# Retention and a mixture of adapters on one core: load tiles on 256-byte addresses, the first quad whole, dummy matmuls while loads are under way

## The chip, the core and the metric

The kernel runs on one core of a Trainium2 chip. The metric is the device time of one execution in microseconds; lower is better. A core has five engines that run side by side and wait for each other through semaphores: TensorE (PE in the rows; its weight loads are PEld) multiplies from SBUF into PSUM, VectorE (DVE), ScalarE (ACT) and GpSimd (POOL) work on elements, and SyncE (SP) issues most of the DMAs that move data between HBM and SBUF. SBUF has 128 partitions; a tile's address is its byte offset in every partition. PSUM is handed out here in eight buffers of one bank each.

## What is computed

Eight sequences (batch) of 576 positions with eight heads of 64 elements go through a masked, decayed product of q, k and v, and the result through a mixture of eight rank-16 adapters, of which each token takes its best two.

```python
scores = scale * np.matmul(q, k.transpose(0, 1, 3, 2))
Dmat = np.where(rel >= 0, gamma[:, None, None] ** rel[None, :, :], 0.0)
ret = scores * Dmat[None, :, :, :]
attn_out = np.matmul(ret, v)                        # (8, 8, 576, 64)
x = attn_out.transpose(0, 2, 1, 3).reshape(4608, 512)
logits = x @ w_gate                                 # (4608, 8)
topk = np.argpartition(-logits, K, axis=1)[:, :K]   # K = 2
w = softmax of the two selected logits
delta[mask] += w[mask, k, None] * ((x[mask] @ A[e]) @ B[e])
return x + delta
```

## The kernel before

The positions are cut into four full chunks of 128 and one half chunk of 64, the eight batches into two quads of four. A full quad and chunk makes two units of two batches each (`units`, line 192), 16 full units in all, and the half chunk two units more, 18. Between chunks a decayed state P carries what k and v have summed up; so the work of a unit is always on 128 positions.

Each quad's q, k and v come as three tiles of 128 positions x (4 batches x 8 heads x 64) floats, 8 KB in each partition, from the pool `io` with three buffers each (`issue`, line 152). In HBM one row of 64 floats, 256 bytes, lies together. Quad 0 is loaded in nine DMAs (line 178): q and k of batch 0, of batch 1, then v of each, then batches 2 and 3 of q, k and v; the constants (`pack`) stand in between. Behind them come the adapter weights (`load_moe`: A in four DMAs of 64-byte pieces, the gate, B on GpSimd's queue), and then quad 1 in three DMAs. Later quads are issued two quads ahead, at the start of the first unit of a quad (line 513). All these DMAs but B, and all stores, are on SP's queue.

The stages of a unit, all written in one order by hand (each engine's `chain`, lines 73 to 87, keeps TensorE, VectorE and ScalarE in program order; GpSimd and SP are left to the scheduler):

- `scale_v` (line 203): GpSimd scales the unit's v in place, two instructions, for the unit after the current one.
- T (line 213): 16 transposes of q and 16 of k into PSUM, copied to `qT` and `kT` by ScalarE, the q of unit 0 by VectorE.
- S (line 268): 32 matmuls kT by qT; VectorE multiplies by the triangular mask into `rt`.
- Q (line 244): 32 matmuls of the state by qT, from chunk 1 on.
- U (line 315): 32 matmuls k by v, the state's update.
- R (line 341): 32 matmuls v by rt; VectorE scales into `xT`.
- Z (line 416): 16 matmuls of xT by `AW`, the adapters' A beside the gate (two versions, AW[1] a copy of AW[0] with its halves exchanged); then the choice of two on VectorE.
- W (line 443): gating on ScalarE and VectorE. B (line 386): 16 transposes of xT back into `po`. X (line 404): transposes of the gated z. Y (line 466): 4 matmuls by B on top of `po`, four copies to `osb` by ScalarE, two stores.

In the steady state TensorE's order in one step is S(t), T(t+1), B(t-1), Q(t), U(t), R(t), X(t-1), Z(t), Y(t-1). The opening is written apart (line 516): for unit 0 T and S are done batch by batch, then U and R; T(1) follows, and GpSimd copies AW[1]. Step 1 is S(1), T(2), U(1), R(1), Z(0), Z(1), and step 2 takes W, B, X and Y of both units 0 and 1. Names in brackets below, as S(2), are a stage and its unit.

Tiles are laid one after another in SBUF in the order of the pools: the constants first, then `io`, `work` and `moe` (which holds `osb`, the tile that stores leave from). Each tile's size is rounded up to 32 bytes; `warm` has 4 bytes and `pack` 464.

Of the kernel before, what the change touches and what calls it, by code (L numbers as in the profile page):

```python
# [18 lines left out]
def kernel(  # L19
# [17 lines left out]
    L = 64  # L37
# [42 lines left out]
    def mm(*args, **kw):  # L80
        chain("pe", nc.tensor.matmul(*args, **kw))  # L81
# [4 lines left out]
    def act(fn, **kw):  # L86
        chain("act", getattr(nc.scalar, fn)(**kw))  # L87

    cpool = ctx.enter_context(tc.tile_pool(name="consts", bufs=1))
    iop = ctx.enter_context(tc.tile_pool(name="io", bufs=3))  # L90
    wk = ctx.enter_context(tc.tile_pool(name="work", bufs=2))
    mo = ctx.enter_context(tc.tile_pool(name="moe", bufs=3))
    pp = ctx.enter_context(tc.tile_pool(name="pp", bufs=8, space=bass.MemoryType.PSUM))
# [22 lines left out]
    for g in range(2):  # L116
        gp.tensor_copy(
            out=trih[64 * g : 64 * g + 64], in_=tri[64 * g : 64 * g + 64, 64 * g : 64 * g + 64]
        )
    warm = cpool.tile([128, 1], FP32, tag="warm", name="warm")  # L120
    nc.vector.memset(warm, 0.0)
    nc.scalar.activation(out=warm, in_=warm, func=AFT.Sigmoid)
    pack = cpool.tile([128, NPK], FP32, tag="pack", name="pack")
# [28 lines left out]
    def issue(n):  # L152
        if n >= len(quads):
            return
        c, qd = quads[n]
        first = n == 0
        tl = [
            iop.tile([128, QUAD, H, Dh], FP32, tag=tag, name=tag) for tag in ("q32", "k32", "v32")
        ]
        if c == NFULL:  # L160
            for src, dst in zip((q, k, v), tl):
                for g in range(2):
                    nc.sync.dma_start(
                        out=dst[64 * g : 64 * g + 64, 0:2].rearrange("p s h d -> p (s h) d"),
                        in_=src[
                            QUAD * qd + 2 * g : QUAD * qd + 2 * g + 2, :, C * c : C * c + L, :
                        ].rearrange("s h j d -> j (s h) d"),
                    )
        def load(n, lo, hi):
            nc.sync.dma_start(  # L170
                out=tl[n][:, lo:hi].rearrange("p b h d -> p (b h) d"),
                in_=(q, k, v)[n][
                    QUAD * qd + lo : QUAD * qd + hi, :, C * c : C * c + C, :
                ].rearrange("b h j d -> j (b h) d"),
            )

        if first:
            for n, lo, hi in ((0, 0, 1), (1, 0, 1), (0, 1, 2), (1, 1, 2), (2, 0, 1), (2, 1, 2)):
                load(n, lo, hi)
                if (n, lo) == (1, 1):  # L180
                    nc.sync.dma_start(out=pack, in_=dr_pack.ap())
            for n in range(3):
                load(n, 2, 4)
            load_moe()
        elif c < NFULL:
            for n in range(3):
                load(n, 0, 4)
        for sl in range(2):
            nat[(c, qd, sl)] = [x[:, 2 * sl : 2 * sl + 2] for x in tl]
# [7 lines left out]
    def rows(g):  # L197
        return slice(64 * g, 64 * g + 64)
# [11 lines left out]
                op=ALU.mult,  # L210
            )

    def stage_T(t, bs=(0, 1)):

        q32, k32, v32 = nat[units[t]]
        s = st.setdefault(t, {})
        n = len(bs)
        for src, nm in ((q32, "qT"), (k32, "kT")):
            if bs[0] == 0:
                s[nm] = wk.tile([128, 2, HP, C], FP32, tag=nm, name=nm)  # L220
            dst = s[nm]
            ps = [pp.tile([128, HP, n, L], FP32, tag="pb", name=f"p{nm}") for _ in range(2)]
            for hp in range(HP):
                for b in bs:
                    for g in range(2):
                        mm(
                            ps[g][:, hp, b - bs[0], :],
                            lhsT=src[rows(g), b, 2 * hp : 2 * hp + 2, :],
                            rhs=id64[rows(g), :],
                            is_transpose=True,  # L230
                            start=True,
                            stop=True,
                        )
            for g in range(2):
                if is_full(t):
                    o = dst[:, bs[0] : bs[-1] + 1, :, rows(g)].rearrange("p b a i -> p a b i")
                else:
                    o = dst[:, g].rearrange("p a (b i) -> p a b i", b=2)
                if t == 0 and nm == "qT":
                    vec("tensor_copy", out=o, in_=ps[g])  # L240
                else:
                    act("copy", out=o, in_=ps[g])
# [22 lines left out]
                            skip_group_check=True,  # L265
                        )

    def stage_S(t, bs=(0, 1)):
        s = st[t]
        rt = s.setdefault("rt", {})  # L270
        if not is_full(t):
            ps = [pp.tile([128, HP, 2, L], FP32, tag="pb", name=f"pe{ho}") for ho in range(2)]
            for hp in range(HP):
                for y in range(2):
                    for x in range(2):
                        for ho in range(2):
                            mm(
                                ps[ho][rows(x), hp, y, :],
                                lhsT=s["kT"][rows(ho), x, hp, rows(y)],
                                rhs=s["qT"][rows(ho), x, hp, rows(y)],  # L280
                                start=(hp == 0 and y == 0),
                                stop=True,
                                skip_group_check=True,
                            )
            for ho in range(2):
                r = wk.tile([128, HP, 2, L], FP32, tag=f"rh{ho}", name=f"rh{ho}")
                vec("tensor_tensor", 
                    out=r.rearrange("p a y i -> p (a y) i"),
                    in0=ps[ho].rearrange("p a y i -> p (a y) i"),
                    in1=trih.unsqueeze(1).broadcast_to((128, HP * 2, L)),  # L290
                    op=ALU.mult,
                )
                rt[ho] = r
            return
        for b in bs:
            ps = [pp.tile([128, HP, C], FP32, tag="pb", name=f"ps{ho}") for ho in range(2)]
            for hp in range(HP):
                for ho in range(2):
                    mm(
                        ps[ho][:, hp, :],  # L300
                        lhsT=s["kT"][rows(ho), b, hp, :],
                        rhs=s["qT"][rows(ho), b, hp, :],
                        start=(hp == 0),
                        stop=True,
                        skip_group_check=True,
                    )
            for ho in range(2):
                r = wk.tile([128, HP, C], FP32, tag=f"rt{ho}", name=f"rt{ho}", bufs=4)
                vec(
                    "tensor_tensor", out=r, in0=ps[ho],  # L310
                    in1=tri.unsqueeze(1).broadcast_to((128, HP, C)), op=ALU.mult,
                )
                rt[(b, ho)] = r
# [152 lines left out]
    def stage_Y(t):  # L466
        c, qd, sl = units[t]
        s = st.pop(t)
        po = s["po"]
        osb = mo.tile([128, 2, HP, 2, Dh], FP32, tag="osb", name="osb", bufs=3)  # L470
        bv = Bcat.rearrange("p (a o d) -> p a o d", a=HP, o=2)
        for cc in range(2):
            for g in range(2):
                mm(
                    po[cc][:, g, :, :],
                    lhsT=s["zT"][:, g, :],
                    rhs=bv[:, :, cc ^ g, :],
                    start=False,
                    stop=True,
                    skip_group_check=True,  # L480
                )
        for cc in range(2):
            for g in range(2):
                act("copy", out=osb[:, g, :, cc ^ g, :], in_=po[cc][:, g])
        of = osb.rearrange("p g a o d -> p g (a o d)")
        for g in range(2):
            for x in range(1 if c < NFULL else 2):
                bt = 2 * sl + g if c < NFULL else 2 * g + x
                n0 = S * (QUAD * qd + bt) + C * c
                if c < NFULL:  # L490
                    nc.sync.dma_start(out=out[n0 : n0 + C, :], in_=of[:, g, :])
                else:
                    nc.sync.dma_start(out=out[n0 : n0 + L, :], in_=of[rows(x), g, :])
# [17 lines left out]
    for t in range(NU):  # L511
# [2 lines left out]
        if t + 1 < NU:  # L514
            scale_v(t + 1)
        if t == 0:
            for b in range(2):
                stage_T(0, (b,))
                stage_S(0, (b,))
            stage_Q(0)  # L520
            stage_U(0)
            stage_R(0)
            stage_T(1)
            for ho in range(2):
                gp.tensor_copy(out=AW[1][rows(ho)], in_=AW[0][rows(1 - ho)])
            continue
        done = [0, 1] if t == 2 else [t - 1] if t > 2 else []
        if not is_full(t):
# [11 lines left out]
        stage_R(t)  # L540
        for u in done:
            stage_X(u)
        if t == 1:
            stage_Z(0)
        stage_Z(t)
        for u in done:
            stage_Y(u)
# [34 lines left out]
```

## Time and profile before

| | us |
|---|---|
| median of 3 runs (lowest to highest) | 216.16 (215.51 to 217.12) |
| the profiled execution, its time | 216.31 |
| the profiled execution, its span | 214.6 |
| TensorE busy in the span | 185.4 (86%) |
| VectorE, ScalarE, GpSimd busy | 108.1, 72.9, 58.3 |
| HBM read, written | 28.91 MB, 9.44 MB |

The span runs from the first to the last instruction of the program; the time holds what lies around it as well. Rows give times in us from the span's start. [...] An engine's busy time is the time its instructions were being worked on; matmuls are pipelined, so that the mean of one is longer than the step from one to the next.

### The profile page before, as it was taken

The numbers are of one execution on the slowest core, as the hardware profiler recorded it, in microseconds if no ns is written. First come the engines' busy times: TensorE is split into PE (matmuls) and PEld (weight loads), VectorE is DVE, ScalarE is ACT, GpSimd is POOL, SyncE is SP. The second block draws the span as 40 slices with busy tenths as digits, with TensorE's granted clock in tenths as the row PEclk, the third lists the DMA queues.
The fourth block names the chain that finished last, engine by engine and source line by source line (L and its number), as shares of the span: only waits on it lengthen the run. The fifth ranks groups of instructions, "written<-read, shape, count | busy, mean of one in ns | idle before, by whom it ended". The sixth has DMA issues, their size and how long they took to land.

```text
span 214.6 us, 8018 instructions
## 1 busy us (share of the span) xinstructions
PE 185.4 (86%) x3564; PEld 169.3 (79%) x3564; DVE 108.1 (50%) x269; ACT 72.9 (34%) x200; POOL 58.3 (27%) x68
## 2 busy tenths in 40 slices
PE   1688328999999989999999998999899999998850
PEld 1577318989998979898989997999799999987730
DVE  0333401576756545756565656555655546443620
ACT  2202122143633333333434342435243525163141
POOL 4353200702504501721180029004732041200000
PEclk9999955999999999999999999999999999999996
DMA  6997999999999989779988698999981642020235
GB/s 137 232 220 87 208 219 219 196 228 205 218 221 322 226 194 215 256 161 233 230 204 224 145 252 193 259 203 230 266 206 46 167 91 99 5 101 3 104 77 118
DMA packets 57010, 38.73 MB, mean 180 GB/s; under 512 B 30736, under 2 KB 52368, under 8 KB 56976
## 3 DMA queue, kind: packets, MB, share of 16 engines
q1 hardware_dynamic: 56832, 38.09, 78.7%
q8 instruction: 28, 0.46, 0.9%
q0 software_dynamic: 144, 0.13, 0.4%
q14 instruction: 6, 0.05, 0.1%
HBM read 28.91 MB, written 9.44 MB: 179 GB/s over the span
## 4 chain that ended last, share of the span: by engine, by line
PE 70%; DMA 10%; SPq 9%; DVE 3%; issue 2%; POOL 2%; ACT 1%; ACTq 0%
PE px L81 19%; PE pz L81 15%; PE ps L81 12%; PE po L81 8%; PE pu L81 8%; SPq L170 6%; DMA k<-in_k_dram 5%; DMA v<-in_v_dram 4%; PE pkT L81 3%; SPq L139 3%; PE pqT L81 3%; POOL v L206 2%; PE pzt L81 2%; DVE rt L84 1%; ACT osb L87 1%
## 5 line engine op out<-in xcount | busy, mean ns | idle before, releaser
L206 POOL TENSOR_TENSOR v<-v,pack 128x512 f32<-128x512 f32 x36 | 36.5, 1043 | 82.0 <-DMA v<-in_v_dram 81.9
L84 DVE TENSOR_TENSOR rt<-ps,tri 128x512 f32<-128x512 f32 x64 | 39.8, 683 | 20.3 <-PE ps L81 20.3
L81 PE MATMUL pz<-AW,xT 128*128 128x136 f32 x288 | 37.2, 283 | 1.1 <-DVE xT L84 1.1
L81 PE MATMUL ps<-qT,kT 64*128 64x128 f32 x512 | 35.0, 288 | 3.7 <-ACT kT L87 2.4
L81 PEld LDWEIGHTS ps<-qT,kT 64*128 64x128 f32 x512 | 31.6, 196 | 7.1 <-ACT kT L87 4.2
L81 PEld LDWEIGHTS pz<-AW,xT 128*128 128x128 f32 x288 | 34.5, 190 | 1.6 <-DVE xT L84 1.5
L81 PE MATMUL px<-rt,v 128*64 128x128 f32 x512 | 33.1, 285 | 0.0
L87 ACT COPY osb<-po 128x256 f32<-128x256 f32 x72 | 21.5, 390 | 30.0 <-PE po L81 30.0
L81 PEld LDWEIGHTS px<-rt,v 128*64 128x64 f32 x512 | 30.0, 145 | 0.0
L87 ACT COPY qT<-pqT 128x512 f32<-128x512 f32 x34 | 18.3, 590 | 33.9 <-PE pqT L81 33.9
L84 DVE TENSOR_TENSOR xT<-px,asc 128x512 f32<-128x512 f32 x36 | 24.7, 691 | 9.5 <-PE px L81 8.4
L339 POOL TENSOR_TENSOR P<-pn,gdec 128x512 f32<-128x512 f32 x12 | 15.2, 1271 | 38.6 <-DVE pn L84 38.6
L87 ACT COPY zT<-pzt 128x256 f16<-128x256 f16 x18 | 6.6, 372 | 54.5 <-PE pzt L81 54.5
L87 ACT COPY kT<-pkT 128x512 f32<-128x512 f32 (+1 forms) x38 | 19.9, 585 | 10.5 <-PE pkT L81 10.5
L81 PE MATMUL pu<-v,k 128*64 128x64 f32 x512 | 20.3, 236 | 2.8 <-issue 1.4
L81 PEld LDWEIGHTS pu<-v,k 128*64 128x64 f32 x512 | 18.0, 148 | 5.7 <-POOL v L206 3.1
L81 PE MATMUL pqT<-id,q 64*128 64x64 f32 x288 | 13.4, 236 | 8.0 <-DMA q<-in_q_dram 8.0
L81 PEld LDWEIGHTS pqT<-id,q 64*128 64x128 f32 x288 | 12.4, 150 | 8.5 <-issue 8.4
L84 DVE TENSOR_TENSOR pn<-pu,P 128x512 f32<-128x512 f32 x12 | 8.3, 692 | 20.2 <-PE pu L81 20.2
L81 PE MATMUL pkT<-id,k 64*128 64x64 f32 x288 | 13.7, 234 | 4.2 <-DMA k<-in_k_dram 4.1
L81 PE MATMUL po<-id,xT 64*128 64x64 f32 x288 | 15.9, 229 | 0.7 <-DVE rt L84 0.3
L81 PE MATMUL px<-qT,P 64*64 64x128 f32 (+1 forms) x512 | 15.9, 261 | 0.6 <-issue 0.6
(39 smaller groups left out, 127.5 us busy)
## 6 DMA issues: line engine op xcount, KB each, us to landing
out_dram<-osb SPq DMA_DIRECT2D x32, 256.0 KB, 3.9
q<-in_q_dram SPq DMA_DIRECT2D x6, 256.0 KB, 5.5
k<-in_k_dram SPq DMA_DIRECT2D x6, 256.0 KB, 4.8
v<-in_v_dram SPq DMA_DIRECT2D x6, 256.0 KB, 4.8
out_dram<-osb SPq DMA_DIRECT2D x8, 128.0 KB, 2.4
q<-in_q_dram SPq DMA_DIRECT2D x1, 512.0 KB, 6.2
k<-in_k_dram SPq DMA_DIRECT2D x1, 512.0 KB, 7.5
v<-in_v_dram SPq DMA_DIRECT2D x1, 512.0 KB, 7.8
```

What stands on the lines that cost most here:

```text
L81: chain("pe", nc.tensor.matmul(*args, **kw))
L84: chain("dve", getattr(nc.vector, fn)(**kw))
L87: chain("act", getattr(nc.scalar, fn)(**kw))
L139: nc.sync.dma_start(out=AW[0][:, dt, 0:ER].rearrange("p (e r) -> p e r", e=E), in_=moe_A[:, 128 * dt : 128 * dt + 128, :].rearrange("e d r ...
L170: nc.sync.dma_start(out=tl[n][:, lo:hi].rearrange("p b h d -> p (b h) d"), in_=(q, k, v)[n][QUAD * qd + lo : QUAD * qd + hi, :, C * c : C ...
L206: nc.gpsimd.tensor_tensor(out=vv[:, b], in0=vv[:, b], in1=gv[:, 0 if is_full(t) else 1].unsqueeze(2).broadcast_to((128, H, Dh)), op=ALU.mult,)
L339: nc.gpsimd.tensor_tensor(out=Pt, in0=pn, in1=gdec, op=ALU.mult)
```

## The change

Two pools are opened ahead of the constants: `padp` with `warm`, now 32 floats instead of 1, and then `io`, followed by a new pool `outp` that holds `osb`. The constants come behind them. Quad 0 is loaded in three DMAs, one for each of q, k and v, with `pack` behind k. T and S lose their form for single batches; the q of unit 1 is copied by VectorE too. `spin` issues dummy matmuls of a zeroed fp16 tile, 128 x 128 by 128 x 512, into a PSUM tile that nothing reads: 12 ahead of T(0) and 12 between its q and its k transposes. The opening is then T(0), T(1), S(0), S(1), U(0), R(0), U(1), R(1), the copy of AW[1], Z(0), Z(1), T(2), and step 1 is empty but for its scaling of v. From step 2 on the order is the same.

```diff
--- before.py
+++ after.py
@@ -86,8 +86,13 @@
     def act(fn, **kw):
         chain("act", getattr(nc.scalar, fn)(**kw))
 
+
+
+    padp = ctx.enter_context(tc.tile_pool(name="padp", bufs=1))
+    warm = padp.tile([128, 32], FP32, tag="warm", name="warm")
+    iop = ctx.enter_context(tc.tile_pool(name="io", bufs=3))
+    outp = ctx.enter_context(tc.tile_pool(name="outp", bufs=3))
     cpool = ctx.enter_context(tc.tile_pool(name="consts", bufs=1))
-    iop = ctx.enter_context(tc.tile_pool(name="io", bufs=3))
     wk = ctx.enter_context(tc.tile_pool(name="work", bufs=2))
     mo = ctx.enter_context(tc.tile_pool(name="moe", bufs=3))
     pp = ctx.enter_context(tc.tile_pool(name="pp", bufs=8, space=bass.MemoryType.PSUM))
@@ -117,7 +122,15 @@
         gp.tensor_copy(
             out=trih[64 * g : 64 * g + 64], in_=tri[64 * g : 64 * g + 64, 64 * g : 64 * g + 64]
         )
-    warm = cpool.tile([128, 1], FP32, tag="warm", name="warm")
+    idle = cpool.tile([128, 512], FP16, tag="idle", name="idle")
+    nc.vector.memset(idle, 0.0)
+    spare = pp.tile([128, 512], FP32, tag="pb", name="spare")
+
+    def spin(n):
+
+        for _ in range(n):
+            mm(spare, lhsT=idle[:, 0:128], rhs=idle, start=True, stop=True)
+
     nc.vector.memset(warm, 0.0)
     nc.scalar.activation(out=warm, in_=warm, func=AFT.Sigmoid)
     pack = cpool.tile([128, NPK], FP32, tag="pack", name="pack")
@@ -175,12 +188,10 @@
             )
 
         if first:
-            for n, lo, hi in ((0, 0, 1), (1, 0, 1), (0, 1, 2), (1, 1, 2), (2, 0, 1), (2, 1, 2)):
-                load(n, lo, hi)
-                if (n, lo) == (1, 1):
+            for n in range(3):
+                load(n, 0, 4)
+                if n == 1:
                     nc.sync.dma_start(out=pack, in_=dr_pack.ap())
-            for n in range(3):
-                load(n, 2, 4)
             load_moe()
         elif c < NFULL:
             for n in range(3):
@@ -210,21 +221,20 @@
                 op=ALU.mult,
             )
 
-    def stage_T(t, bs=(0, 1)):
+    def stage_T(t, pause=0):
 
         q32, k32, v32 = nat[units[t]]
         s = st.setdefault(t, {})
-        n = len(bs)
         for src, nm in ((q32, "qT"), (k32, "kT")):
-            if bs[0] == 0:
-                s[nm] = wk.tile([128, 2, HP, C], FP32, tag=nm, name=nm)
-            dst = s[nm]
-            ps = [pp.tile([128, HP, n, L], FP32, tag="pb", name=f"p{nm}") for _ in range(2)]
+            if nm == "kT":
+                spin(pause)
+            dst = s[nm] = wk.tile([128, 2, HP, C], FP32, tag=nm, name=nm)
+            ps = [pp.tile([128, HP, 2, L], FP32, tag="pb", name=f"p{nm}") for _ in range(2)]
             for hp in range(HP):
-                for b in bs:
+                for b in range(2):
                     for g in range(2):
                         mm(
-                            ps[g][:, hp, b - bs[0], :],
+                            ps[g][:, hp, b, :],
                             lhsT=src[rows(g), b, 2 * hp : 2 * hp + 2, :],
                             rhs=id64[rows(g), :],
                             is_transpose=True,
@@ -233,10 +243,10 @@
                         )
             for g in range(2):
                 if is_full(t):
-                    o = dst[:, bs[0] : bs[-1] + 1, :, rows(g)].rearrange("p b a i -> p a b i")
+                    o = dst[:, :, :, rows(g)].rearrange("p b a i -> p a b i")
                 else:
                     o = dst[:, g].rearrange("p a (b i) -> p a b i", b=2)
-                if t == 0 and nm == "qT":
+                if t < 2 and nm == "qT":
                     vec("tensor_copy", out=o, in_=ps[g])
                 else:
                     act("copy", out=o, in_=ps[g])
@@ -265,7 +275,7 @@
                             skip_group_check=True,
                         )
 
-    def stage_S(t, bs=(0, 1)):
+    def stage_S(t):
         s = st[t]
         rt = s.setdefault("rt", {})
         if not is_full(t):
@@ -292,7 +302,7 @@
                 )
                 rt[ho] = r
             return
-        for b in bs:
+        for b in range(2):
             ps = [pp.tile([128, HP, C], FP32, tag="pb", name=f"ps{ho}") for ho in range(2)]
             for hp in range(HP):
                 for ho in range(2):
@@ -467,7 +477,7 @@
         c, qd, sl = units[t]
         s = st.pop(t)
         po = s["po"]
-        osb = mo.tile([128, 2, HP, 2, Dh], FP32, tag="osb", name="osb", bufs=3)
+        osb = outp.tile([128, 2, HP, 2, Dh], FP32, tag="osb", name="osb")
         bv = Bcat.rearrange("p (a o d) -> p a o d", a=HP, o=2)
         for cc in range(2):
             for g in range(2):
@@ -514,15 +524,22 @@
         if t + 1 < NU:
             scale_v(t + 1)
         if t == 0:
-            for b in range(2):
-                stage_T(0, (b,))
-                stage_S(0, (b,))
-            stage_Q(0)
-            stage_U(0)
-            stage_R(0)
+            spin(12)
+            stage_T(0, pause=12)
             stage_T(1)
+            stage_S(0)
+            stage_S(1)
+            for u in range(2):
+                stage_Q(u)
+                stage_U(u)
+                stage_R(u)
             for ho in range(2):
                 gp.tensor_copy(out=AW[1][rows(ho)], in_=AW[0][rows(1 - ho)])
+            for u in range(2):
+                stage_Z(u)
+            stage_T(2)
+            continue
+        if t == 1:
             continue
         done = [0, 1] if t == 2 else [t - 1] if t > 2 else []
         if not is_full(t):
@@ -540,8 +557,6 @@
         stage_R(t)
         for u in done:
             stage_X(u)
-        if t == 1:
-            stage_Z(0)
         stage_Z(t)
         for u in done:
             stage_Y(u)
```

## Rows read from the trace of the kernel before

**Rows 1.** Busy time by engine in stretches: engines, PEclk, DMA share, GB/s.
```profile
0.00:19.60 19.60, 12.46 (x138) 11.21 (x140) 5.80 (x12) 2.78 (x6) 8.63 (x22) 1.00 1.03 180
19.60:26.50 6.90, 2.95 (x60) 2.62 (x56) 2.82 (x5) 2.05 (x4) 2.22 (x3) 1.00 0.91 168
26.50:36.70 10.20, 5.03 (x76) 4.78 (x78) 0.69 (x1) 2.15 (x4) 0.00 (x0) 0.50 1.11 218
36.70:41.90 5.20, 5.20 (x58) 4.90 (x54) 2.79 (x6) 0.24 (x2) 4.04 (x4) 1.00 0.98 193
41.90:205.00 163.10, 157.85 (x3223) 144.68 (x3222) 94.80 (x239) 62.57 (x175) 43.45 (x40) 1.00 0.76 183
```

**Rows 2.** The chain that ended last: start us, us, what.
```profile
21.28 11.37 DMA k<-in_k_dram
```

**Rows 3.** TensorE's timeline, opening: start, us, operation xcount [idle before <-releaser].
```profile
4.20 0.69 PE L81 MATMUL pqT<-id,q 64*128 64x64 f32 x8 [4.20 <-DMA q<-in_q_dram]
5.28 0.69 PE L81 MATMUL pkT<-id,k 64*128 64x64 f32 x8 [0.39 <-DMA k<-in_k_dram]
6.70 2.08 PE L81 MATMUL ps<-qT,kT 64*128 64x128 f32 x16 [0.73 <-ACT kT L87]
...
15.49 3.63 PE L81 MATMUL px<-rt,v 128*64 128x128 f32 x32
...
27.96 1.12 PE L81 MATMUL pqT<-id,q 64*128 64x64 f32 x16 [3.78 <-DMA q<-in_q_dram]
32.79 1.12 PE L81 MATMUL pkT<-id,k 64*128 64x64 f32 x16 [3.71 <-DMA k<-in_k_dram]
...
41.89 2.06 PE L81 MATMUL ps<-qT,kT 64*128 64x128 f32 x32
...
46.94 1.15 PE L81 MATMUL pu<-v,k 128*64 128x64 f32 x32
```

**Rows 4.** Stretches chosen for the DMA traffic, columns as in rows 1.
```profile
2.00:4.00 2.00, 0.00 (x0) 0.00 (x0) 0.00 (x0) 0.29 (x2) 1.30 (x4) 1.00 1.01 229
...
17.00:22.00 5.00, 3.50 (x52) 3.02 (x50) 1.38 (x2) 1.98 (x4) 2.38 (x3) 1.00 0.64 60
...
23.00:24.00 1.00, 1.00 (x22) 0.99 (x18) 0.68 (x2) 0.00 (x0) 0.00 (x0) 1.00 1.04 293
24.00:26.00 2.00, 0.19 (x4) 0.00 (x0) 1.81 (x4) 0.00 (x0) 0.00 (x0) 1.00 1.11 219
...
68.00:70.00 2.00, 2.00 (x38) 1.83 (x34) 1.52 (x3) 0.00 (x0) 2.00 (x3) 1.00 1.03 361
```

**Rows 5.** One steady unit in the chain that ended last.
```profile
61.73 0.44 PE po L81 x4
62.17 1.99 PE ps L81 x32
64.16 0.50 PE pqT L81 x16
...
66.98 1.08 PE pu L81 x32
68.06 1.75 PE px L81 x32
...
70.03 1.91 PE pz L81 x16
```

**Rows 6.** The timeline of ScalarE and VectorE, opening.
```profile
20.98 1.09 ACT L87 COPY kT<-pkT 128x512 f32<-128x512 f32 x2
...
23.32 2.48 DVE L84 TENSOR_TENSOR rt<-ps,tri 128x512 f32<-128x512 f32 x4 [3.39 <-PE ps L81]
```

**Rows 7.** GpSimd's timeline, opening.
```profile
18.51 2.04 POOL L206 TENSOR_TENSOR v<-v,pack 128x512 f32<-128x512 f32 x2 [4.62 <-DMA v<-in_v_dram]
```

**Rows 8.** TensorE's waits, 42 to 205 us: waited for, us, times, longest.
```profile
PE pu L81 <- issue: 1.4, 3, 0.7
...
PE pu L81 <- POOL v L206: 0.9, 1, 0.9
```

## The prediction

> **What bounds the kernel now.** I cut the span by stages first [rows 1]. From 41.9 to 205.0 us TensorE is busy for 157.85 of 163.1 us at the full granted clock: that stretch is bound by TensorE, one unit after the other, and only 5.2 us in it are idle. Before 41.9 it is busy for 12.46 of 19.6, 2.95 of 6.9 and 5.03 of 10.2 us. The first fifth of the span is where time lies.
>
> The chain that ended last says what this opening waits for [rows 2]: from 21.28 to 32.66 us it is the load of k of the second quad. In TensorE's own order [rows 3] unit 2's q transposes start at 27.96 and its k transposes at 32.79, each when its load lands, and unit 1's second half (U, R), both Z and S(2) follow them. S(2) starts at 41.89. Everything behind S(2) is the same program in both kernels, so I forecast where S(2) starts and shift the rest.
>
> The loads are not waiting to be issued: they run at a plateau. The stretch 24 to 26 us moves 219 GB/s with the DMA engines' share at 1.11, while stores of 2 KB rows move 361 GB/s in 68 to 70 us [rows 4]. So the engines can do more than the loads get from them. The load pieces are 256 B (one row of 64 floats).
>
> The clock is the third part. S(0)'s first half (16 matmuls, half of S) takes 2.08 us at 6.70, and S(2), with 32, takes 2.06 at 41.89; R(0) takes 3.63 us [rows 3], R in the steady stretch 1.75 [rows 5]. [...]
>
> **The change part by part.** All sums are against the profiled execution: span 214.6 us, time 216.31, so 1.7 us lie around the span; it is 0.15 above the median 216.16.
>
> *Addresses.* Summing the tile sizes (each rounded up to 32 B), the q, k and v tiles of before start 128 B past a multiple of 256, osb 224 B past; after, both pools start on multiples. A 256 B piece then no longer lies across two 256 B blocks. No row shows an aligned load. From below it gains nothing: 219 GB/s. From above it is the stores' 361. Just after an idle stretch the same unaligned loads ran at 293 GB/s (23 to 24 us) before they fell to the plateau [rows 4]: reading and sending can go that fast until something behind them fills. I take 293, the row between. A tensor of a quad (4 batches x 8 heads x 128 rows x 256 B = 1.049 MB) then takes 3.6 us, against 4.8 at 219 and 2.9 at 361. For osb I take nothing: stores are off the chain except in the last 9 us, with no row to price them.
>
> [...]
>
> *First quad whole.* Data starts at 2.0 us. The first 256 KB at 229 GB/s [rows 4] are over at 3.15, and TensorE starts on them at 4.20 [rows 3]: 1.05 us from last byte to use. Six small and three larger loads become three. q is usable at 2.0 + 3.6 + 1.05 = 6.6 and k at K = 10.2 (before, first halves at 4.20 and 5.28). With the pack (0.2) v is usable at 14.0. The 64 B pieces of A and the gate follow; before, that stretch (17 to 22 us) moved 60 GB/s [rows 4], and I charge the same 5.0 us. Then q, k, v of quad 1 are usable at 22.7, 26.3, 29.8.
>
> *Stage by stage.* Prices at the full clock come from one steady unit [rows 5]: T 0.5 for q and as much for k, S 2.0, U 1.1, R 1.75, Z 1.9. From K on TensorE has T(0)k and T(1) (1.5); S(0) then waits for the kT copies (1.1 on ScalarE, [rows 6]): start K + 2.0. S(0), S(1): to K + 6.0. U, R, U, R (5.7): K + 11.7. Two Z: K + 15.5. T(2): K + 16.5. New here: S(2) now stands right behind T(2), where before U(1), R(1) and Z hid T(2)'s copies; two pairs of 1.1 us on ScalarE, the first pair half covered, make S(2) K + 18.3 = 28.5.
>
> What must be ready beside it. VectorE: eight masks of 0.62 us (2.48 for four, [rows 6]) end by K + 8, R(1) needs them from K + 9.9; hidden. POOL: scaling a unit takes 2.04 us [rows 7], so v of unit 0 is ready at 14.0 + 2.0 = 16.1, and U(0) wants it at K + 6.0 = 16.2: no room, any us later is a us on the end. AW's copy ends near 20.4, Z(0) wants it at 21.9. T(2) wants k at 26.2 and has it at 26.3. U(2) comes 5.05 us after S(2) [rows 3], at 33.6, and v of quad 1 is scaled for it at 31.9. The DMAs moved on SP's queue (pack ahead of v, the MoE loads behind) keep their order against quad 1; the stores come later and are passed by nothing.
>
> *Keeping the array busy.* A 128-row fp16 matmul of 256 columns costs 0.11 us (0.44 for four, [rows 5]), so 512 columns 0.22, at the lower level 0.44. Twelve from about 1.3 us on at the lower level end at 6.6, just when q lands: free. Twelve more behind T(0)q, 2.6 us at the full clock, end at 9.9 before K: free. If the clock is still low they end near 13 and T(0)k is 2.8 us late.
>
> *Sum.* S(2) at 28.5 for 41.9: 13.4 us. In the TensorE-bound stretch the idle time ahead of U is 1.4 us ("issue") and 0.9 (scaled v) [rows 8]; lighter DMA traffic may take some of it: between 0 and 2.3, I take 1.0. Span 214.6 - 13.4 - 1.0 = 200.2, time 201.9; the 0.15 to the median is inside its spread. Forecast 202.0. At 361 GB/s K is 8.9, S(2) 27.2, with all 2.3 us: 199.3.
>
> What is late next: nothing on the DMA side. A quad's loads (10.8 us) and its stores (1.05 MB at 361: 2.9) fill 14 of the 21 us that two units take, and TensorE is the bound to the end.
>
> **The rivals.**
> 1. *Loads no faster.* For: no row of a load above 293, the plateau may be HBM's. Against: the stores' 361, and the overshoot after idling. Then K is 12.7, v scaled at 19.8, Z(1) done at 29.3, and T(2) waits for k at 32.79 as now, there being the same bytes ahead of it. S(2) 0.5 + 1.1 + 0.2 later, 34.6: 7.3 us gained, no stall removed. Time 209.0.
> 2. *The first dummies don't raise the clock*, and it rises near 19.6 as it seems to do now. For: rows of 0 to 19 us at half speed [rows 3] through several us of work. Against: that work was broken by waits up to 13 us. Price: 2.8 us for the second dozen, and 6.6 us of wall to 19.6 that do half the work, 3.3. Time 208.
> 3. *Slower: the clock stays low through the whole opening.* [...] For: 26.5 to 36.7 us at 0.50 [rows 1]. Against: that fall followed waits for loads, and after K the new order has none over 1 us.
>
> The change not doing what it says would be rival 1 (addresses) or 2 (array).
>
> **How the numbers follow.** Forecast 0.66, holding 199.3 (and a little under, 198.5, for the tail's stores) to 204.5; rival 1 0.15; rival 2, whole or in part, 0.12; rival 3 0.05; within 1%, the bound of what a measurement of this kernel can tell from no change, 0.02, by half of rival 3. Faster by over 1%: 0.66 + 0.15 + 0.12 = 0.93. The range from 198.5 to 208.5 holds the forecast and rival 2, and leaves out rival 3 and most of rival 1.
>
> **What would show it.** Right: load stretches of the opening near 290 GB/s with the DMA share not above now; T(0)k near 10, S(1) over by 17, S(2) near 28.5; S at 2.0 us for 32 matmuls from the first one; no clock row at 0.50 between 10 and 195 us; POOL's scaling of unit 0 ending near U(0)'s start; 41.9 to 205 repeated 13 us earlier with under 5 us idle. Wrong: a plateau of 219 again and S(2) tied to k's landing at 33 (rival 1); S(0) at 4 us (rivals 2, 3); or a new wait in the steady stretch, above all on osb, a PSUM buffer or scaled v.

## The result and the profile after

| | before | after |
|---|---|---|
| median, us (lowest to highest) | 216.03 (215.51 to 217.12) | 204.17 (203.81 to 206.74) |
| profiled execution: time, span | 216.31, 214.6 | 203.81, 202.1 |
| S(2) starts at | 41.89 | 29.82 |
| S(2) to the end of the span | 172.7 | 172.3 |
| DMA queue of loads and stores, share of 16 engines' span | 78.7% | 66.0% |

The ratio of the times is 0.947, 95% interval [0.9385, 0.9555]: 11.9 us less, where 14 were forecast, inside the range. Ratios, here and below, are formed from undisturbed executions alone, so the quotient of two medians can differ from them a little. Of the profiled span's 12.5 us, 12.1 come from the earlier start of S(2) and 0.4 from behind it.

TensorE's timeline of the opening (start, us, operation, tiles xcount, idle before and its releaser) answers to [rows 3]:

```profile
1.26 5.30 PE L81 MATMUL spare<-idle 128*128 128x512 f16 x12 [1.26 <-DVE warm L134]
7.17 0.71 PE L81 MATMUL pqT<-id,q 64*128 64x64 f32 x16 [0.60 <-DMA q<-in_q_dram]
7.82 2.76 PE L81 MATMUL spare<-idle 128*128 128x512 f16 x12
11.25 0.71 PE L81 MATMUL pkT<-id,k 64*128 64x64 f32 x16 [0.67 <-DMA k<-in_k_dram]
...
13.12 3.84 PE L81 MATMUL ps<-qT,kT 64*128 64x128 f32 x64
...
17.67 1.04 PE L81 MATMUL pu<-v,k 128*64 128x64 f32 x28 [0.43 <-POOL v L217]
...
27.66 0.71 PE L81 MATMUL pkT<-id,k 64*128 64x64 f32 x16
29.82 2.06 PE L81 MATMUL ps<-qT,kT 64*128 64x128 f32 x32 [1.45 <-ACT kT L87]
```

The first dozen dummies take 5.30 us, 0.44 each, the second 2.76: the whole first dozen ran at half the speed of the second, though the profile's clock row says 1.00 there (2 to 6 us, below), and full speed was reached by T(0)'s q (0.71 us for 16 transposes, where 16 of k take 1.12 in the run without dummies below). Both S together (64 matmuls) take 3.84 us, where the first half of S(0) alone took 2.08 before. From 11.25 to S(2) TensorE waits once for scaled v (0.43) and once for T(2)'s copies (1.45).

The stretches chosen for the DMA traffic and the long one that answers to the last row of [rows 1] (engines, PEclk, which is the granted TensorE clock as a share of the full one, DMA share, GB/s):

```profile
2.00:4.00 2.00, 2.00 (x6) 0.76 (x5) 0.00 (x0) 0.32 (x2) 1.31 (x4) 1.00 0.64 133
4.00:6.00 2.00, 2.00 (x7) 0.61 (x4) 0.00 (x0) 0.00 (x0) 0.00 (x0) 1.00 1.07 338
6.00:7.00 1.00, 0.56 (x2) 0.00 (x0) 0.00 (x0) 0.00 (x0) 0.00 (x0) 1.00 1.23 255
...
24.00:26.00 2.00, 2.00 (x20) 2.00 (x19) 0.57 (x4) 0.00 (x0) 0.00 (x0) 1.00 1.08 338
...
29.80:195.00 165.20, 158.63 (x3240) 145.32 (x3240) 96.56 (x242) 64.29 (x182) 47.46 (x44) 1.00 0.64 189
```

The same load stretch, 24 to 26 us, moves 338 GB/s for 219 in [rows 4], at nearly the same share of busy engines (1.08 for 1.11). The traffic is no longer even: it starts slowly (133 GB/s in 2 to 4 us, 229 before) and dips between two loads (255). TensorE is still the bound behind S(2), with 6.6 of 165.2 us idle.

What TensorE waited for over the whole span (us in total, times, longest):

```profile
PE po L81 <- DVE zc L84: 1.6, 1, 1.6
PE ps L81 <- ACT kT L87: 1.4, 1, 1.4
...
PE pu L81 <- DVE zc L84: 1.0, 1, 1.0
...
PE pkT L81 <- DMA k<-in_k_dram: 0.7, 1, 0.7
```

Two waits for `zc`, VectorE's gated z (1.6 and 1.0 us), stand where I had none in the sum. The "issue" waits ahead of U of [rows 8] are gone.

### The profile page after: what moved, and what is told of

The parts are those of the page before. It is cut to its first block, busy times and chain, and to the rows that moved or that the text cites. A ratio compares the mean times of both kernels' runs of the same rounds, so it can differ in the third digit from the quotient of the medians.

```text
span 202.1 us, 8056 instructions
## 1 busy us (share of the span) xinstructions
PE 184.5 (91%) x3588; PEld 164.6 (81%) x3588; DVE 109.4 (54%) x270; ACT 71.5 (35%) x196; POOL 58.3 (29%) x68
## 2 busy tenths in 40 slices
DMA packets 47698, 38.73 MB, mean 192 GB/s; under 512 B 18352, under 2 KB 43056, under 8 KB 47664
## 4 chain that ended last, share of the span: by engine, by line
PE 79%; DVE 7%; SPq 4%; DMA 3%; ACT 2%; POOL 1%; issue 1%; ACTq 0%; POOLq 0%
PE px L81 22%; PE pz L81 17%; PE ps L81 13%; PE po L81 9%; PE pu L81 9%; PE pkT L81 3%; PE pqT L81 3%; DMA v<-in_v_dram 3%; DVE rt L84 2%; SPq L183 2%; DVE cm L84 2%; SPq L194 2%; PE pzt L81 2%; POOL v L217 1%; ACT osb L87 1%
## 5 line engine op out<-in xcount | busy, mean ns | idle before, releaser
L81 PE MATMUL ps<-qT,kT 64*128 64x128 f32 x512 | 32.6, 278 | 1.6 <-ACT kT L87 1.4
L81 PEld LDWEIGHTS ps<-qT,kT 64*128 64x128 f32 x512 | 29.7, 188 | 4.6 <-PE po L81 2.7
L81 PE MATMUL px<-rt,v 128*64 128x128 f32 x512 | 30.8, 273 | 0.0
L81 PEld LDWEIGHTS px<-rt,v 128*64 128x64 f32 x512 | 27.8, 137 | 0.0
L87 ACT COPY kT<-pkT 128x512 f32<-128x512 f32 x36 | 19.6, 608 | 9.7 <-PE pkT L81 9.7
L81 PE MATMUL pu<-v,k 128*64 128x64 f32 x512 | 18.6, 225 | 1.4 <-DVE zc L84 1.0
L81 PEld LDWEIGHTS pu<-v,k 128*64 128x64 f32 x512 | 16.4, 138 | 3.9 <-issue 3.1
L84 DVE COPY lg<-pz 128x16 f32<-128x16 f32 x18 | 3.1, 174 | 25.8 <-PE pz L81 25.8
L81 PEld LDWEIGHTS po<-id,xT 64*128 64x128 f32 x288 | 12.1, 139 | 4.4 <-DVE rt L84 2.4
L81 PEld LDWEIGHTS px<-qT,P 64*64 64x64 f32 x512 | 12.5, 133 | 1.3 <-issue 0.4
```

The costliest lines, as they stand in the source:

```text
L84: chain("dve", getattr(nc.vector, fn)(**kw))
```

## The experiments

My theory at this point: the addresses set the load rate, the rate moves every landing of the opening, and order and dummies turn early landings into an early S(2). The main rival: one of the three parts is the whole gain. Each run is compared with the kernel before on the same chip. All runs of this section but four were made on one chip, those four on a second; the changed kernel's 204.17 us don't come from the first, and what that does to the comparisons is said behind the run on the stores' tile.

**The addresses undone.** Everything else stays; the pad ahead of `io` grows by 128 B.

```diff
-    warm = padp.tile([128, 32], FP32, tag="warm", name="warm")
+    warm = padp.tile([128, 64], FP32, tag="warm", name="warm")
```

> The changed kernel with the load and store tiles moved 128 B past a multiple of 256, all else kept. Theory (the addresses set the load rate, and the rate feeds the new opening): loads back at a plateau near 219 GB/s, k of quad 0 usable near 12.7, T(2) waiting for k of quad 1 near 32.8, S(2) near 34.6, time near 209. Rival (the order and the dummies gave the gain, the rate was never what counted): S(2) stays near 30, time near 204.5.

Measured: 213.63 us (211.09 to 214.72), ratio 0.9884 [0.9802, 0.9966]. Its loads while k of quad 0 comes in, and T(2)'s wait for k:

```profile
10.00:12.00 2.00, 2.00 (x7) 0.75 (x6) 0.87 (x2) 0.00 (x0) 0.00 (x0) 0.57 1.11 217
```

```profile
33.80 0.89 PE L81 MATMUL pkT<-id,k 64*128 64x64 f32 x16 [2.28 <-DMA k<-in_k_dram]
```

The rival falls: without the addresses, order and dummies keep 2 us of the 12. It is worse than the 209 I gave. Is it the 128 B, or any offset? The same edit with 40 floats puts the tiles 32 B past:

> The changed kernel with the load tiles and osb 32 B past a multiple of 256 instead of on it. Theory (a piece pays for lying across two 256 B blocks, whatever the offset): the load plateau near 219 GB/s as with 128 B, time as there, 211 to 214. Rival (the cost grows with the part on the far side): a plateau between 219 and 340, time between.

Measured: 211.19 us (210.37 to 215.69), ratio 0.9786 [0.9744, 0.9829], 1% below 128 B off, with intervals that touch. Its stretches, with the stretch at half clock:

```profile
10.00:12.00 2.00, 2.00 (x6) 0.67 (x5) 0.87 (x2) 0.00 (x0) 0.00 (x0) 0.50 1.12 219
...
24.00:26.00 2.00, 2.00 (x50) 2.00 (x48) 1.66 (x3) 0.00 (x0) 0.25 (x1) 1.00 1.11 236
...
35.10:41.90 6.80, 5.61 (x72) 5.57 (x72) 3.04 (x5) 2.73 (x8) 2.74 (x3) 0.50 1.10 220
```

and its TensorE around S(2):

```profile
34.43 0.71 PE L81 MATMUL pkT<-id,k 64*128 64x64 f32 x16 [3.49 <-DMA k<-in_k_dram]
36.33 3.78 PE L81 MATMUL ps<-qT,kT 64*128 64x128 f32 x32 [1.19 <-ACT kT L87]
```

In 10 to 12 us the loads move 219 GB/s, with 128 B off 217: a quarter of the offset came with as low a rate. T(2) waits 3.49 us for k, as rival 1 said. Of the 2.3 us above its 209, 1.7 are S(2)'s later start (36.33 for 34.6, k coming at 34.43 for 32.79), and 0.6 stand behind it. What I had left out as well is what followed the wait: the granted clock is 0.50 for 6.8 us (35.1 to 41.9), and S(2) takes 3.78 us instead of 2.06.

**The addresses alone.** The kernel before with only the pools moved (`padp`, `io` and `outp` ahead of the constants).

> The kernel before with the pools placed as after, nothing else. Theory: loads at 340 GB/s bring k of quad 1 near 26.5 instead of 32.8; U(1), R(1), both Z follow it (9.1 us now, 7.2 at the full clock), S(2) at 34 to 36, time 208 to 210, so that addresses alone give half of the whole and the rest needs the order and the clock. Rival (addresses are the whole gain): 204 to 205. Rival (without the order they give nothing): 215 to 216.

Measured: 209.07 us (208.56 to 210.17), ratio 0.9718 [0.9665, 0.9772], 6.5 us of the 11.9. Its TensorE:

```profile
28.06 0.71 PE L81 MATMUL pkT<-id,k 64*128 64x64 f32 x16 [2.92 <-DMA k<-in_k_dram]
...
29.85 3.41 PE L81 MATMUL px<-rt,v 128*64 128x128 f32 x32
...
37.09 2.06 PE L81 MATMUL ps<-qT,kT 64*128 64x128 f32 x32
```

k of quad 1 is usable 4.7 us earlier than before, and S(2) starts 4.8 us earlier: the chain behind that landing is the same. R(1) takes 3.41 us after the wait for k, R in the steady stretch 1.75. By these medians order and dummies (with the whole first quad) are worth 2.0 us with the loads off the multiple and 4.9 with the loads on it, addresses 6.5 in the old opening and 9.5 in the new; the larger number of each pair leans on the changed kernel's run on another chip, and the comparison on one chip below doesn't show that the parts do more together than apart.

The rate of the first quad is not the addresses' alone. From 4 to 10 us, with quad 0 coming in, the rows are, in this order, of the kernel before, of this run, of the run 128 B off, and of the changed kernel; the last row is this run's quad 1, which is loaded whole in both kernels:

```profile
4.00:10.00 6.00, 4.31 (x48) 3.78 (x48) 1.88 (x4) 0.99 (x4) 1.18 (x2) 1.00 1.20 225
4.00:10.00 6.00, 4.17 (x48) 3.60 (x47) 2.38 (x6) 1.29 (x4) 1.63 (x2) 1.00 1.08 232
4.00:10.00 6.00, 3.70 (x26) 1.45 (x24) 0.41 (x1) 0.00 (x0) 0.00 (x0) 1.00 1.12 240
4.00:10.00 6.00, 5.40 (x34) 2.22 (x32) 1.29 (x2) 0.00 (x0) 0.00 (x0) 1.00 1.09 317
...
22.00:23.00 1.00, 1.00 (x22) 1.00 (x20) 0.12 (x1) 0.00 (x0) 0.00 (x0) 1.00 1.11 337
```

Addresses alone (232) or whole DMAs alone (240) leave quad 0 near the old 225; both together give 317, and the quad that was whole before gains by the addresses alone. The profile counts 30,736 packets under 512 B in the kernel before and in this run, 18,352 in the changed kernel; the difference, 12,384, is close to quad 0's 12,288 rows of 256 B. No run takes the whole first quad back alone, so its share of the time stays open.

**The order undone**, with addresses, whole quad and dummies kept:

```diff
             stage_T(0, pause=12)
-            stage_T(1)
             stage_S(0)
-            stage_S(1)
-            for u in range(2):
-                stage_Q(u)
-                stage_U(u)
-                stage_R(u)
+            stage_Q(0)
+            stage_U(0)
+            stage_R(0)
+            stage_T(1)
...
```

> The changed kernel with its addresses, whole first quad and dummies, but unit 0 worked to its end before T(1), and step 1 as before. Theory (stage by stage fills the wait for scaled v with unit 1's T and S): U(0) still at 17.7, S(0) over near 15, 2.5 us idle ahead of U(0), then T(1), S(1), T(2), U(1), R(1), Z, Z behind: S(2) near 34, time near 208.5. Rival (TensorE's work is the same, order is worth under a microsecond): 204 to 205.

Measured: 207.89 us (206.92 to 209.79), ratio 0.9664 [0.958, 0.9747]: 3.7 us above the changed kernel's median on the other chip.

```profile
13.81 3.56 PE L81 MATMUL ps<-qT,kT 64*128 64x128 f32 x32 [1.16 <-ACT kT L87]
17.73 0.34 PE L81 MATMUL pu<-v,k 128*64 128x64 f32 x4 [0.35 <-POOL v L217]
...
35.11 2.06 PE L81 MATMUL ps<-qT,kT 64*128 64x128 f32 x32
```

The place is right, S(2) at 35.11 for 34 forecast, and the mechanism only in part. Around the first matmuls of U(0) only 0.35 and 0.67 us are idle, because S(0) itself took 3.56 us: TensorE had waited 1.39 us for T(0)'s k and, with T(1) gone from there, 1.16 for its copies, and from 14.1 to 17.5 us the granted clock is 0.50. In the run on the stores' tile below, T(0)'s k made TensorE wait 1.84 us, but T(1) followed, and 64 matmuls of S took 3.84 us: in these two executions S ran at half speed where the wait ahead of it was left open, and at full speed where T(1) filled it.

**The dummies left out.**

```diff
-            spin(12)
-            stage_T(0, pause=12)
+            stage_T(0)
```

> The changed kernel without the 24 dummy matmuls. Theory (the dummies raise the clock before data lands): T, S, U at half speed from 11.3 to somewhere between 17 and 20, S(2) 3 to 4.5 us later than 29.8, time 207 to 208.7. Rival (the opening waits for loads anyway): within 0.7 us of 204.2.

Measured: 205.95 us (204.03 to 207.29), ratio 0.9537 [0.9461, 0.9612]; the interval overlaps the changed kernel's, so the 1.8 us are not clear of noise. The profiled execution shows a loss at S(2):

```profile
11.99 1.12 PE L81 MATMUL pkT<-id,k 64*128 64x64 f32 x16 [3.52 <-DMA k<-in_k_dram]
...
14.60 4.21 PE L81 MATMUL ps<-qT,kT 64*128 64x128 f32 x64
...
31.21 2.06 PE L81 MATMUL ps<-qT,kT 64*128 64x128 f32 x32 [1.19 <-ACT kT L87]
```

T is slower (1.12 us for 16 transposes of k against 0.71), but 64 matmuls of S are over in 4.21 us against 3.84: full speed was reached within S, with no wait of TensorE since 11.99. S(2) starts 1.4 us later, 0.7 of them because k itself was later in this execution; yet the span ends at 202.3 for 202.1, because the waits for `zc` behind S(2) happened to be shorter (1.5 us for 2.6). So no gain of the dummies in time is shown. My 3 to 4.5 us took the clock's rise from the kernel before, where the work was broken by waits.

**The stores' tile alone.** osb goes back into its old pool (64 B past a multiple), the loads stay.

> The changed kernel with only osb moved back into the pool it came from, 64 B past a multiple of 256; q, k, v stay on multiples. Theory (only the loads' 256 B pieces matter; a store moves 2 KB rows and is off the chain): within 0.6 us of 204.2. Rival (stores gain as well): 1 to 3 us more, seen as a lower rate where stores run alone and a longer last 9 us.

Measured: 206.04 us (203.34 to 206.35), ratio 0.9542 [0.9487, 0.9597], on another chip than the changed kernel's run. So it was run once more beside the changed kernel:

> The changed kernel with only osb off the multiple of 256, once more beside the changed kernel on one chip, as the first time the two stood on different chips. If stores matter: 1 us or more above the changed kernel of this call. If only loads do: within 0.6 us of it.

> The changed kernel as it is, beside the three others of this call on one chip: 203.5 to 205, for a comparison without the chip between.

Measured on that chip: 204.49 us (202.5 to 206.5), ratio 0.9392 [0.934, 0.9444], against 203.77 (202.63 to 205.35), ratio 0.9395 [0.9352, 0.9438], for the changed kernel. No effect that these runs can tell; one of several tenths is not excluded.

These two runs also change how the others read. The same kernel has the ratio 0.9542 [0.9487, 0.9597] on the first chip and 0.9392 [0.934, 0.9444] on the second: 1.5%, or 3 us, lie between the two occasions. The changed kernel itself was not run on the first chip, so the kernel with only osb moved is its nearest stand-in there. Against it, by the ratios, the addresses are worth 7.4 us in the new opening (0.9884) and 6.1 in the old, the order 2.6 (0.9664, with intervals that overlap by 0.2%), and the dummies nothing (0.9537). Order, whole quad and dummies together are worth 2.5 us with the loads off the multiple and 3.8 with the loads on it, a difference inside the intervals.

**The new wait in W.** In the changed kernel the gating comparison `cm` of unit 0 (VectorE) lies beside GpSimd's scaling of quad 1:

```profile
31.29 4.05 POOL L217 TENSOR_TENSOR v<-v,pack 128x512 f32<-128x512 f32 x4 [10.29 <-DMA v<-in_v_dram]
...
33.41 1.95 DVE L84 SCALAR_TENSOR_TENSOR cm<-lg,m,sg 128x8 f32<-128x8 f32 x2
L84 DVE SCALAR_TENSOR_TENSOR cm<-lg,m,sg x2: 954/1015/1076, 33.4 to 34.3; 128x8 f32<-128x8 f32 x2
...
35.69 0.35 DVE L84 SCALAR_TENSOR_TENSOR cm<-lg,m,sg 128x8 f32<-128x8 f32 x2
```

The first pair takes 1.95 us and ends as GpSimd ends (35.34), the second pair, for unit 1, 0.35. The third line is the first pair taken apart: two instructions of 0.95 and 1.08 us, each over with one of GpSimd's last two scalings, which are 1.01 us apart. `cm` reads `lg` and `sg` from SBUF; `lg` is a copy of what lies in PSUM. That the reads from SBUF tie the pair to GpSimd's scalings was my guess from these times, and the next run takes one of the two away:

```diff
-                out=cm[:, g, :], in0=lg[:, g, :], scalar=m8[:, g, 1:2], in1=sg[:, g, :],
+                out=cm[:, g, :], in0=pz[:, g, ER : ER + E], scalar=m8[:, g, 1:2], in1=sg[:, g, :],
```

> The changed kernel where the gating comparison in W reads the logits where Z left them in PSUM instead of the SBUF copy, so that this VectorE instruction has one SBUF tensor fewer. Theory (VectorE's W(0) stood still from 33.4 to 35.3 us because GpSimd was scaling v from 31.3 to 35.3, and B(1) waited 1.6 us for it): the pair takes 0.35 us there, B(1)'s wait falls under 0.6 us, and so does the wait ahead of U of unit 12; time 1 to 2.5 us less than 204.2. Rival (the pair waits for something else, or the mask of VectorE is what holds): the pair keeps its 1.9 us, time unchanged within 0.5 us.

Measured: 202.83 us (200.87 to 204.57), ratio 0.9384 [0.9333, 0.9435]; the interval still overlaps the changed kernel's on the other chip, but lies clear below the stand-in's on this one (0.9542 [0.9487, 0.9597]). Whether the pair still ends with the scalings, GpSimd and VectorE of this run tell:

```profile
32.73 4.05 POOL L217 TENSOR_TENSOR v<-v,pack 128x512 f32<-128x512 f32 x4 [10.92 <-DMA v<-in_v_dram]
...
34.45 0.35 DVE L84 SCALAR_TENSOR_TENSOR cm<-pz,m,sg 128x8 f32<-128x8 f32 x2
```

In the midst of the same GpSimd work the pair takes 0.35 us, for 1.95 with `lg` read from SBUF, and neither wait for `zc` in the steady stretch is left. From S(2) to the end the span has 169.4 us for 172.3.

This also reads the waits ahead of U in the kernel before anew, 0.9 us for scaled v and 1.4 for "issue" in [rows 8]. Its VectorE and its TensorE at those four places:

```profile
87.06 1.15 DVE L84 SCALAR_TENSOR_TENSOR cm<-lg,m,sg 128x8 f32<-128x8 f32 x2
...
107.90 1.21 DVE L84 SCALAR_TENSOR_TENSOR cm<-lg,m,sg 128x8 f32<-128x8 f32 x2
...
128.80 1.54 DVE L84 SCALAR_TENSOR_TENSOR cm<-lg,m,sg 128x8 f32<-128x8 f32 x2
...
150.04 1.72 DVE L84 SCALAR_TENSOR_TENSOR cm<-lg,m,sg 128x8 f32<-128x8 f32 x2
```

```profile
88.71 1.15 PE L81 MATMUL pu<-v,k 128*64 128x64 f32 x32 [0.36 <-issue]
...
109.61 1.15 PE L81 MATMUL pu<-v,k 128*64 128x64 f32 x32 [0.37 <-issue]
...
130.84 1.15 PE L81 MATMUL pu<-v,k 128*64 128x64 f32 x32 [0.71 <-issue]
...
152.26 1.15 PE L81 MATMUL pu<-v,k 128*64 128x64 f32 x32 [0.89 <-POOL v L206]
```

All four stand behind the same slowed pair, beside GpSimd's scalings from 87.10, 107.04, 127.27 and 147.69; a longer pair goes with a longer wait, and unit 12's own v had been scaled 20 us before. That the pair held TensorE there is inferred from these times; the changed kernel's row for the same kind of wait names `zc`.

**k from another queue.** Two loads on one queue left a dip between them (255 GB/s in 6 to 7 us).

```diff
-            nc.sync.dma_start(
+            eng = nc.scalar if first and n == 1 else nc.sync
+            eng.dma_start(
```

> The changed kernel with the load of k of quad 0 issued from ScalarE's queue, all else from SP. Theory (k was usable 1 us later than worked out because SP started its issue 1.3 us after q's and the traffic fell off between the two, not because the rate is lower): k of quad 0 usable near 10.3 instead of 11.25, v and the rest with it, S(2) near 28.9, time 0.5 to 1 us less than 204.2. Rival (k is bound by the rate): k usable at 11.25, or later if q and k share the engines, no gain.

Measured: 207.19 us (205.11 to 209.44), ratio 0.9594 [0.9547, 0.9642]: no gain, as the rival had it. It is 3 us above the changed kernel's median on the other chip; against the stand-in on this one (0.9542) the intervals overlap. Its DMA in 6 to 8 us, then its TensorE:

```profile
6.00:8.00 2.00, 0.56 (x2) 0.00 (x0) 0.00 (x0) 0.00 (x0) 0.00 (x0) 1.00 1.12 330
```

```profile
10.88 1.12 PE L81 MATMUL pqT<-id,q 64*128 64x64 f32 x16 [4.31 <-DMA q<-in_q_dram]
11.93 5.18 PE L81 MATMUL spare<-idle 128*128 128x512 f16 x12
17.04 0.72 PE L81 MATMUL pkT<-id,k 64*128 64x64 f32 x16
```

The dip is gone, and q, with k's load under way beside it, is usable at 10.88 instead of 7.17. TensorE idles 4.31 us, behind that T(0)'s q takes 1.12 us instead of 0.71, and the second dozen, 5.18 us now for 2.76, delays T(0)'s k by itself.

**Towards a better version**, on the second chip. The `cm` edit with 18 dummies ahead of T(0)'s k:

> The changed kernel with the gating comparison read from PSUM and 18 instead of 12 dummies between T(0)'s q and k. Theory for the first edit as before (1 to 2.5 us off, B(1)'s wait gone). For the second: k of quad 0 has landed between 11.25 and 12.3 us in the runs so far, the second dozen ends at 10.5, and a drop of the clock after such a gap is what separates the slower executions from the faster; 18 dummies end near 11.9, so no clock row at 0.50 before the tail and a median nearer to the fastest: 201 to 202. Rival (the drops have another cause, or the longer pause only delays T(0)k): median 202.8 or more.

Measured: 202.69 us (201.65 to 204.54), ratio 0.9344 [0.9298, 0.939]; the changed kernel on the same chip had 0.9395 [0.9352, 0.9438]. It is 1.1 us better by the medians, with overlapping intervals, and not told apart from the `cm` edit alone. The theory on the clock falls in its place: a drop came all the same, later.

```profile
30.20:33.50 3.30, 3.30 (x36) 3.30 (x36) 1.29 (x2) 0.43 (x3) 1.78 (x2) 0.50 1.02 276
```

This one follows the wait ahead of S(2) (1.19 us); S(2) takes 3.60 us in it. The changed kernel's own second profile has one from 35.7 to 39.1 us, behind the waits in B; its first profile has none. Last, that gap filled: T(2)'s q copied by VectorE, B(0) between T(2) and S(2).

> The two edits of the run before, and the gap between T(2) and S(2) filled: T(2)'s q copied by VectorE, B(0) moved from step 2 into the gap. Theory (1.2 to 1.6 us of TensorE idle there are the copies of T(2) on ScalarE): S(2) starts 0.4 us earlier or the wait ahead of it falls to 0.5, and B's 0.7 us no longer stand behind S(2); 0.5 to 1 us less than the run before, 200.5 to 201.5. Rival (PSUM buffers held by po make S(2) or T(3) wait): no gain, or slower by up to 1 us.

Measured: 204.36 us (201.9 to 205.38), ratio 0.9394 [0.9343, 0.9444], 1.7 us worse than the run before by the medians, with overlapping intervals.

```profile
32.00 2.06 PE L81 MATMUL ps<-qT,kT 64*128 64x128 f32 x32 [0.70 <-ACT kT L87]
...
34.54 0.71 PE L81 MATMUL pqT<-id,q 64*128 64x64 f32 x15 [0.33 <-DVE rt L84]
```

The wait ahead of S(2) fell to 0.70, and T(3) now waits twice 0.33 us for VectorE's masks, as the rival had it with PSUM buffers held by `po`. That is at most 0.7 of the 1.7; k of quad 0 and of quad 1 were late in this profile, and why, stays open.

## Why the prediction was right, point by point

- **K, k of quad 0 usable: 10.2 forecast, 11.25.** That the addresses would speed up the loads was right (338 GB/s for 219 in 24 to 26 us), though for quad 0 only together with its whole DMAs. Why a piece off the multiple costs rate no run here shows, nor that anything fills behind the loads, as the sum had it for their fall from 293 to 219. (The tile sizes alone add up to a multiple of 256; the 128 B of the prediction's sum need the four small constants that the trace shows being set ahead of all pools, 32 B each after rounding.) The term "3.6 us a tensor at 293 GB/s" was mis-sized in two ways that nearly cancel. The plateau is 338, better than the 293 I took, which is 1.0 us less for q and k. But the first 2 us moved 133 GB/s, not the 229 of the small loads: 0.41 MB short of the plateau, 1.2 us; and the dip between the loads costs 0.25. That is half of the miss, and that it is no more is luck. The other half no row here places; it may lie between the last byte and its use, for which I took 1.05 us from a load a quarter as large, and it is within what executions differ by: the changed kernel's second profile has k usable at 10.71, the run on the stores' tile at 12.34, with the same loads.
- **K to S(2): 18.3 forecast, 18.6.** The stage prices of one steady unit at the full clock held. The place with "no room", U(0) behind v's scaling, cost 0.43 us: v came late by more than k, its scaling starting at 15.57 for 14.0.
- **S(2): 28.5 forecast, 29.82.** The miss of 1.3 us is K's 1.05 and 0.3 in the chain.
- **The stalls behind S(2): 1.0 forecast to go, 0.4 went.** This is the step that failed in kind. I let lighter DMA traffic take the "issue" waits and the late v; by the reading above all 2.3 us go with VectorE's `cm` beside GpSimd. They went where the scalings no longer met W, one of 1.0 us was left, and an earlier S(2) brought W(0) under the scaling of quad 1 and added a stall of 1.6 us. The two misses, 1.3 and 0.6, are the difference between the forecast span of 200.2 and 202.1.
- **Rival 1** was given 209.0; with the tiles off, it is 211 to 214. The wait for k was the right one, but k came 1 to 1.6 us later than 32.79, and what followed the wait was not in the sum: S(2) took 3.78 us for 2.06 in both runs with the tiles off.
- **Rival 2** did not happen: the second dozen took 2.76 us. The lower level in its sums is half the full speed, as the dozens show it, 0.44 us a dummy and then 0.23. Its price of 6 us was too high: without any dummies S(2) came 1.4 us later, full speed being reached within S, and no loss in time is clear of noise, so the dummies are the part for which no gain is shown.
- **Rival 3** did not happen: in the profile of after no clock row is at 0.50 between 6.8 us and 195.

## What to carry to other kernels

A load in small pieces can be bound by where its pieces land (here 219 GB/s, and 338 once the tiles were moved): if its plateau is far below what long rows reach on the same engines (here 361), look at the tile's offset and at the size of the DMAs before the queue. Price an order at the landing times it will have, and count for every wait of TensorE also the half-speed stretch that may follow it (3.3 to 6.8 us here, in some executions). A wait named after one engine's counter can belong to another: look whether the named work had long been done, and whether an instruction nearby takes several times its usual time. Run the changed kernel again on every chip on which its parts are run: here the same kernel differed by 1.5% between two.

## What the hardware did that I had not expected

With an offset of 32 B the loads were as slow as with one of 128 B, 219 and 217 GB/s in 10 to 12 us, where tiles on the multiple moved 338 (4 to 6 and 24 to 26 us). Beside GpSimd's scalings, 1.04 us each and back to back, each of the two `cm` instructions of unit 0 was over only with the scaling it met: the pair took 1.95 us, for 0.35 in unit 1 and, with the logits read from PSUM, in unit 0 too. And waits of TensorE of 1.2 to 1.6 us, a few microseconds apart, were in some executions followed by 3.3 to 3.4 us at a granted clock of 0.50 (the order undone; 18 dummies; the changed kernel's second profile) and in others not (its first profile; the `cm` edit alone). Whether these drops make the spread between executions stays open: the changed kernel's first four fall in order, 203.81 us at a mean granted clock of 0.990 to 206.74 at 0.966, but of the six on the second chip 205.35 had 0.982 and 203.65 had 0.977.
